# Multi-query attention with a SiLU feed-forward on one core: w1's load moved behind the transposes of x, the prologue replanned, other last rows for ScalarE and VectorE

## The chip, the core and the metric

The kernel runs on one core of a Trainium2 chip. The engines that matter here are TensorE (PE in the profile), VectorE (DVE), ScalarE (ACT), GpSimd (POOL) and SyncE (SP), which issues nearly all transfers. Each engine works through its own list of instructions in order, and the lists are tied together by semaphores. The metric is the device time of one execution in microseconds (us), as the median of several runs.

## The reference

The input x has 2048 rows of 640 columns. It is normalised by row, and the result feeds two branches whose outputs are added to x. Branch A is attention with 32 query heads of 20 columns and one shared key and value head; branch B is a feed-forward network with 1728 hidden columns.

```python
xn = _layernorm(x)                                   # (x - mean) / sqrt(var + 1e-5)
q = (xn @ wq).reshape(B, S, H, Dh).transpose(0, 2, 1, 3)
k, v = xn @ wk, xn @ wv                              # one head of 20 for all 32
p = softmax(einsum("bhqd,bkd->bhqk", q, k) * Dh ** -0.5)
o = einsum("bhqk,bkd->bhqd", p, v)
A = o.transpose(0, 2, 1, 3).reshape(B, S, H * Dh) @ wo
Bv = silu(xn @ w1) @ w2
out = x + A + Bv
```

## The kernel before

**Tiling.** The 2048 rows are 16 tiles of 128 rows (NT) and 4 chunks of 512 queries (QC). The scores of one head, one chunk of queries and one tile of 128 keys are a block of 128 keys by 512 queries; there are 32 x 4 x 16 = 2048 blocks. They are taken in groups of four heads (GB = 64 blocks), key tile by key tile, head by head inside a key tile. PE makes three (sometimes four) blocks at once (do_S, L1049, matmul L1101), each in one of PSUM's eight banks.

**Two ways to the exponential.** Most blocks go to ScalarE, which takes two or three banks in one instruction (L1135; here called a pair of 1024 columns, a triple of 1536, a single of 512). The others go to VectorE, which makes of the scores an integer whose bits are an approximate exponential (p1, L1150); two shifted copies of it are added by GpSimd (L1187) or VectorE (L1181), three blocks at a time. A block of ScalarE then costs one product with v on PE, a block of VectorE three (L942). Which blocks go to VectorE is decided block by block from its backlog (pick_dve, L974).

**Other work.** Once the sums of a group are complete, VectorE copies them out (L1231), a transfer transposes them (L1200), and VectorE and GpSimd divide by the row sums (L1215, L1220). Beside all this PE runs what is called jobs: q products for later heads (qd_job, L1268, followed by small transfers at L1290), hidden products of the feed-forward network with w1 (h_job, L1302, then tanh on ScalarE at L1324 and a product on VectorE at L1329), and output products (out_job, L1366). Products of this kind with 32 columns of weights are run four side by side (mm4, L840, matmul L844); four of them are called a quad here.

**What sets the order.** All of it is laid out when the kernel is built, by a list scheduler written in the kernel (Sched, L217). It knows a duration for each operation and a latency for each engine, and keeps a clock per engine; at each step the engine that is free first takes the ready operation of the best priority (run, L319; commit, L294). PE has its own choice (step, L683): scores if three banks are free, products with v, a job, or filler matmuls on zeros (fill, L784, matmul L820) that keep it busy. The result is one fixed list for each engine, and semaphore waits where an operation needs another engine's result (emit, L362). The row SEG (L115) sets the thresholds of these choices anew for every 32 blocks. The scheduler's times only decide the order; on the chip each engine goes on as soon as its waits are met.

**The prologue** (L1504). SP issues the loads of x, tile by tile (L1520), then wq (L1541), then w1 in five pieces (L1543), then transfers that transpose normalised tiles 4, 5 and 7 to 15 (L1704, "xTd"); then a fill of q's layout (qz, L1716) and the residual rows (L1461). The statistics of tiles 0, 4, 6, 9, 11 and 14 are made by ScalarE in two passes (L1610, L1613), the others by VectorE (L1625 twice, L1627). Three batches (tiles 0 to 3, 4 to 9, 10 to 15) each get a chain of small Newton operations on VectorE for 1/sqrt (newton, L1654), whose last operation makes -mean/std (L1683); a tile is then normalised as x * rstd + nb (norm, L1643) by VectorE, ScalarE (L1645) or GpSimd (L1650), as NORM_ENG says. Tiles 0 to 3 and 6 are transposed on PE (tr_job, L1735) and copied by ScalarE (0 and 2, L1747) or VectorE (L1750). k is made for two tiles at a time (k_job, L1754, copied by VectorE at L1766; GpSimd makes a second form of it for VectorE's blocks, L1768), v for four (v_job, L1773). The first q product, for four heads and 512 queries, is one job (q_job, L1246), copied by ScalarE (L1258). The jobs' order is the string PRO after a fixed start: four transposes, q, two k.

**The end.** The last chunk's output rows are four tiles in two halves each. For the first NEARLY tiles an earlier sum (the feed-forward part, x and the first columns of the attention output) is kept in SBUF, and VectorE adds the last products to it (L1412). For the other tiles, and the first HELD ones, a PSUM bank is held with the products made so far (hold_job, L1437); of the other tiles ScalarE copies the finished bank out (L1409). All need the last group, which is transposed on PE (L1238), normalised and copied (oT_last_job, L1350, copy L1361).

Of the kernel before, what the change touches and what calls it, by code (L numbers as in the profile page):

```python
# [15 lines left out]
P = 128  # L16
# [3 lines left out]
DC = 5  # L20
# [40 lines left out]
NEARLY = 3  # L61
EK = 3
HELD = 2
# [31 lines left out]
DVE_FROM = 3  # L95
NODB = 2
# [8 lines left out]
PRO = "v0 t6 k2 k3 v1 k4 q1 k5 v2 k6 k7 v3 d0"  # L105
ACT_STATS = (0, 4, 6, 9, 11, 14)
NW_ENG = ("dve", "dve", "dve")
NORM_ENG = ("pool", "pool", "pool", "pool", "dve", "dve", "act", "act", "pool", "pool", "act", "pool")
# [5 lines left out]
            "ACT4", "SPLIT", "U2")  # L114
SEG = (  # L115
    (4.7587, 0.6558, 0.636, 0.0937, 9, 3, 0, 1.3, 0.05, 0.63, 4.5, 24, 0.91, 1.3294, 10, 21, 8, 54, 22, 27, 99, 0, 0, 0, 99),
    (4.7587, 0.6558, 0.61, 0.112, 9, 3, 0, 1.3, 0.05, 0.6, 0.06, 24, 0.44, 1.3294, 0, 21, 8, 54, 24, 27, 99, 0, 0, 0, 99),
    (4.7587, 1.786, 0.633, 0.153, 7, 5, 3, 1.33, 0.05, 2.36, 0.03, 37, 2.01, 0.4, 10, 6, 5, 54, 15, 99, 99, 0, 0, 0, 99),
    (4.7587, 1.675, 0.488, 0.153, 7, 5, 3, 2.06, 0.05, 0.61, 0.03, 37, 2.01, 0.55, 10, 6, 5, 54, 15, 99, 99, 0, 0, 0, 99),
    (4.7587, 1.675, 0.633, 0.153, 7, 5, 3, 2.06, 0.05, 0.61, 0.03, 37, 2.01, 0.55, 10, 6, 5, 54, 15, 33, 99, 0, 0, 0, 99),  # L120
    (3.659, 1.675, 0.467, 0.034, 7, 5, 1, 1.98, 0.05, 0.41, 0.03, 34, 2.01, 0.55, 10, 6, 12, 54, 16, 33, 99, 0, 0, 0, 99),
    (3.659, 1.675, 0.576, 0.034, 7, 5, 1, 1.98, 0.05, 0.41, 0.03, 34, 2.01, 0.55, 10, 6, 12, 54, 16, 33, 99, 0, 0, 0, 99),
    (4.7587, 1.675, 0.633, 0.153, 7, 5, 3, 2.06, 0.05, 0.61, 0.03, 37, 3.09, 0.55, 10, 6, 5, 54, 15, 33, 99, 0, 0, 0, 99),
    (4.7587, 1.675, 0.633, 0.153, 7, 3, 3, 2.06, 0.05, 0.61, 0.03, 29, 3.09, 0.55, 10, 6, 5, 54, 15, 33, 9, 0, 0, 0, 99),
    (4.7587, 1.482, 0.633, 0.129, 9, 3, 1, 1.33, 0.05, 2.27, 4.5, 24, 0.89, 2.045, 10, 6, 7, 54, 22, 27, 99, 0, 0, 0, 99),
    (4.197, 0.657, 0.708, 0.288, 3, 1, 7, 0.02, 0.05, 4.23, 2.77, 26, 2.57, 1.233, 10, 7, 6, 54, 22, 99, 99, 0, 0, 0, 99),
# [57 lines left out]
class Op:  # L184
# [3 lines left out]
    def __init__(self, eng, dur, fn, deps, prio=0.0, name="", on_sched=None, mode=None):  # L188
# [21 lines left out]
        self.late = 0.0  # L210


LAT = {"pe": 0.215, "act": 0.238, "dve": 0.14, "pool": 0.19, "sp": 0.0}
INF = float("inf")


class Sched:  # L217
# [76 lines left out]
    def commit(self, op, start):  # L294
# [3 lines left out]
        if op.dma:  # L298
            if op.name in ("oTd", "xTd", "uTd"):
                self.dma_t = op.end  # L300
# [1570 lines left out]
```

## Time and profile before

| what | us |
| --- | --- |
| three runs | 683.74, 683.84, 687.07 |
| median | 683.84 |
| the profiled execution, its own time | 686.08 |
| its span, from the first to the last instruction | 684.3 |
| busy in the span: PE, ScalarE, VectorE, GpSimd | 673.0, 667.2, 610.8, 570.0 |
| exponentials on ScalarE (L1135), 649 instructions | 637.0 |
| blocks that VectorE takes (L1150), 687 | 456.5 |
| granted PE clock, mean | 0.994 |

The profile is of one execution. Busy time is the time in which an engine had an instruction at work; neighbours overlap, so a busy time over the count is more than the distance from one to the next. "Idle before" an instruction is shown with what ended it. The profiled execution took 686.08 us, of which 684.3 are the span and 1.8 lie around it.

### The profile page before, as it was taken

What the parts mean: (1) busy time and instruction counts of PE and PEld (TensorE: products, weight loads), DVE (VectorE), ACT (ScalarE), POOL (GpSimd) and SP (SyncE); (2) the same over time, 40 slices, a digit from 0 to 9 for tenths busy, and PEclk for the clock granted to TensorE, in tenths of its full rate; (3) what the DMA queues carried; (4) which work ended last, traced back from release to release, by engine and by line L of the source; (5) the groups of instructions that cost most, each with busy time, mean ns of one, the idle gap of its engine ahead of it and who ended that gap; (6) DMA issues with size and microseconds to landing.
All of it is one profiled execution on the core that took longest, in us unless ns stands there. A gap on an engine that the chain in (4) does not pass through costs nothing.

```text
span 684.3 us, 22554 instructions
## 1 busy us (share of the span) xinstructions
PE 673.0 (98%) x9632; PEld 225.2 (33%) x9634; DVE 610.8 (89%) x1088; ACT 667.2 (98%) x740; POOL 570.0 (83%) x450
## 2 busy tenths in 40 slices
PE   9799999999999999999999999999999999999997
PEld 4332222333323322333323322333332332233333
DVE  7689999888999998989999889988999999898996
ACT  7899999999999999999999999999999999999995
POOL 3567899789989999997798999899777998887692
PEclk9899999999999999999999999999999999999999
DMA  9735400000103100000002310000101220000101
GB/s 265 163 99 146 140 10 15 2 12 16 17 10 91 51 10 18 10 10 18 17 2 53 78 30 10 17 2 17 13 15 34 70 56 2 16 11 17 26 10 40
DMA packets 52728, 28.03 MB, mean 41 GB/s; under 512 B 38582, under 2 KB 51990, under 8 KB 52630
## 3 DMA queue, kind: packets, MB, share of 16 engines
q1 hardware_dynamic: 51174, 26.38, 15.2%
q8 instruction: 77, 1.26, 0.8%
q10 hardware_dynamic: 1456, 0.22, 0.2%
q14 instruction: 21, 0.17, 0.1%
HBM read 11.44 MB, written 2.62 MB: 21 GB/s over the span
## 4 chain that ended last, share of the span: by engine, by line
PE 65%; ACT 30%; DVE 3%; DMA 1%; issue 0%; POOL 0%; SPq 0%; DVEq 0%
ACT sbt L1135 28%; PE psall L942 23%; PE psall L1101 21%; PE psall L844 20%; ACT sbt L1324 2%; DVE sbt L1625 1%; DMA sbt<-sbt 1%; PE psall L1758 1%; DMA sbt<-in_A_x_dram 1%; PE psall L1314 0%; DVE sbt L1150 0%; POOL sbt L1650 0%; DVE sbt L1412 0%; DVE sbt L1650 0%; DVE sbt L1766 0%
## 5 line engine op out<-in xcount | busy, mean ns | idle before, releaser
L1135 ACT ACTIVATE sbt<-psall 128x1024 bf16<-128x1024 f32 (+1 forms) x649 | 637.0, 1177 | 4.8 <-PE psall L1101 4.1
L1187 POOL TENSOR_TENSOR sbt<-sbt 128x768 int32<-128x768 int32 x373 | 529.3, 1447 | 83.8 <-DVE sbt L1181 57.1
L1150 DVE TENSOR_SCALAR sbt<-psall 128x512 int16<-128x512 f32 x687 | 456.5, 685 | 51.9 <-PE psall L1101 44.0
L942 PE MATMUL psall<-sbt 128*32 128x512 bf16 x3422 | 265.1, 383 | 0.1
L1101 PE MATMUL psall<-sbt 32*128 32x512 bf16 x2048 | 252.8, 385 | 2.4 <-ACT sbt L1135 0.5
L844 PE MATMUL psall<-sbt 128*32 128x320 bf16 (+1 forms) x3903 | 231.9, 333 | 0.8 <-DVE sbt L1766 0.5
L1101 PEld LDWEIGHTS psall<-sbt 32*128 32x128 bf16 x2048 | 66.7, 91 | 249.0 <-issue 97.3
L844 PEld LDWEIGHTS psall<-sbt 128*32 128x32 bf16 x3903 | 81.9, 95 | 86.1 <-issue 62.2
L942 PEld LDWEIGHTS psall<-sbt 128*32 128x32 bf16 x3422 | 67.2, 95 | 99.4 <-issue 68.8
L1181 DVE TENSOR_SCALAR sbt<-sbt 128x1536 int16<-128x1536 int16 (+1 forms) x93 | 52.4, 574 | 0.2
L1324 ACT ACTIVATE sbt<-psall 128x512 bf16<-128x512 f32 x54 | 39.6, 732 | 0.0
L1329 DVE SCALAR_TENSOR_TENSOR sbt<-sbt,psall 128x512 bf16<-128x512 bf16 x54 | 37.0, 685 | 2.5 <-ACT sbt L1324 2.0
L1220 POOL TENSOR_TENSOR sbt<-sbt 128x320 bf16<-128x320 bf16 x31 | 22.6, 729 | 2.4 <-DVE sbt L1181 2.2
L1231 DVE CAST sbt<-psall 128x512 bf16<-128x512 f32 x32 | 21.8, 682 | 0.5 <-PE psall L942 0.3
L820 PE MATMUL psall<-sbt 128*128 128x512 bf16 (+3 forms) x53 | 15.7, 449 | 2.5 <-DVE sbt L1564 1.2
L1650 POOL TENSOR_SCALAR sbt<-sbt 128x640 bf16<-128x640 bf16 x7 | 6.0, 876 | 13.9 <-DVE sbt L1683 13.9
L1412 DVE SCALAR_TENSOR_TENSOR sbt<-psall,sbt 128x320 bf16<-128x320 f32 x30 | 14.1, 483 | 2.4 <-PE psall L844 2.3
L1281 DVE TENSOR_SCALAR sbt<-psall 128x512 bf16<-128x512 f32 (+1 forms) x19 | 12.9, 681 | 0.5 <-PE psall L844 0.5
L1393 DVE SCALAR_TENSOR_TENSOR sbt<-psall,sbt 128x320 bf16<-128x320 f32 x26 | 12.5, 482 | 0.8 <-PE psall L844 0.8
L1625 DVE BATCH_NORM_STATS2 sbt<-sbt 128x6 f32<-128x320 bf16 x20 | 9.2, 476 | 3.3 <-DMA sbt<-in_A_x_dram 3.3
L820 PEld LDWEIGHTS psall<-sbt 128*128 128x128 bf16 x55 | 6.0, 113 | 9.9 <-issue 4.0
L1758 PE MATMUL psall<-sbt 128*128 128x256 bf16 x40 | 7.0, 308 | 1.7 <-DMA sbt<-sbt 1.1
(71 smaller groups left out, 92.1 us busy)
## 6 DMA issues: line engine op xcount, KB each, us to landing
sbt<-in_A_x_dram SPq DMA_DIRECT2D x32, 160.0 KB, 3.4
out_dram<-sbt SPq DMA_DIRECT2D x15, 160.0 KB, 1.9
sbt<-in_B_w_dram SPq DMA_DIRECT2D x5, 432.0 KB, 6.7
sbt<-sbt SPq DMA_DIRECT2D x105, 20.0 KB
sbt<-in_B_w_dram SPq DMA_DIRECT2D x13, 160.0 KB, 3.2
sbt<-sbt SPq DMA_DIRECT2D x1, 1024.0 KB, 6.6
sbt<-sbt SPq DMA_TRANSPOSE x58, 2.5
sbt<-in_A_wo_dram SPq DMA_DIRECT2D x5, 160.0 KB, 3.1
```

What stands on the lines that cost most here:

```text
L820: return pe.matmul(self.bk(b, 0, n), self.zero[:, 0:P], self.zero[:, 0:n], start=True, stop=True)
L844: ins = pe.matmul(self.bk(b, 0, n, r, r + SLOT), w[:, r:r + SLOT], x, start=start, stop=stop, tile_position=(0, r), skip_group_check=True)
L942: ins = pe.matmul(self.bk(ub[k], 0, QW, r, r + SLOT), self.v[:, it.w, it.kt, :], it.x(), start=f, stop=False, tile_position=(0, r), skip_g ...
L1101: ins = pe.matmul(self.bk(bank[x]), self.kT[r:r + SLOT, kk, kt * P:(kt + 1) * P], self.qT[r:r + SLOT, g % 8, (g // 8) % 2, :], start=True, ...
L1135: return a.activation(self.E[:, b0 * QW:(b0 + na) * QW].rearrange("p (b n) -> p b n", n=QW), src, AF.Exp, scale=ACT_SCALE)
L1150: return v.tensor_scalar(self.Z[:, zs, zp * QW:(zp + 1) * QW], self.bk(bb), 0.0, ZMAX, ALU.max, ALU.min)
L1181: sc.new("dve", td, lambda v, k=k: v.tensor_scalar(self.Y[:, zs, k, 0:w], self.Z[:, zs, 0:w], float(PH[k + 1][0]), None, ALU.add), zk, yk, ...
L1187: sc.new("pool", tp, lambda v, k=k, cb=cb: v.tensor_tensor(self.Y[:, zs, k, 0:w].bitcast(I32), self.Z[:, zs, 0:w].bitcast(I32), cb, ALU.ad ...
L1220: op = sc.new(eng, 0.75 if eng == "pool" else t_dve_ps(16 * DH), lambda v: v.tensor_tensor(dst, ut[:, :, :, 0:DH], rb, ALU.mult), [key, (" ...
L1231: sc.new("dve", t_dve_ps(QW), lambda v: v.tensor_copy(self.U[:, up, :], self.bk(ub)), [("B", ub)], [("U", up)], prio=U_PRIO, name=f"Uev{g}")
L1324: sc.new("act", t_act(QW), lambda a: a.activation(t, src, AF.Tanh, scale=0.5), [("B", b)], [("tb", tp)], prio=TH_PRIO, name=f"th{c}_{fk}")
L1329: sc.new("dve", t_dve_ps(QW), lambda v: v.scalar_tensor_tensor(out=self.hT[0:rows, fk, :], in0=t, scalar=1.0, in1=src, op0=ALU.add, op1=AL ...
```

## The change

- w1's five loads go out on SP's queue after the transposes of x and the fill of q, instead of before them (load_w1).
- The string PRO now holds the whole order of the first jobs: two transposes, the first k product, two transposes, the first q product in two halves of 256 queries ("p0", "p1") with the second k product between them. k's product 4 stands ahead of v's second one.
- Tile 8 is normalised by GpSimd instead of VectorE, tile 12 by VectorE instead of GpSimd. VectorE and GpSimd normalise as (x - mean) * rstd; the operation that makes -mean/std is left out in batches of which ScalarE normalises no tile. The first norm is tied to the end of the first Newton chain.
- The scheduler's assumptions: a time for each transfer by its queue (dmaq), a start time for each engine, PE's latency 0.222 instead of 0.215, a later result for tanh, 0.69 for GpSimd's normalisation. A setting LOOK lets an engine hold off for an operation of better priority; it is 0 in all rows of SEG.
- Of the last chunk two tiles (four half rows) are finished by ScalarE and two by VectorE, instead of one and three; no held banks for the first tiles.
- Most rows of SEG have other values.

In the built kernel the blocks divide into 1364 for ScalarE (579 pairs, 68 triples, 2 singles) and 684 for VectorE; before, 1361 (576, 68, 5) and 687. The long run of work between prologue and end has another order throughout.

```diff
 H_FIRST = 4
-NEARLY = 3
+NEARLY = 2
 EK = 3
-HELD = 2
+HELD = 0
...
 DVE_FROM = 3
+Q0_SPLIT = 1
+W1_LATE = 1
...
 PV_GO = 9
-PRO = "v0 t6 k2 k3 v1 k4 q1 k5 v2 k6 k7 v3 d0"
+PRO = "t0 t1 k0 t2 t3 p0 k1 p1 v0 t6 k2 k3 k4 v1 q1 k5 v2 k6 k7 v3 d0"
...
 NW_ENG = ("dve", "dve", "dve")
-NORM_ENG = ("pool", "pool", "pool", "pool", "dve", "dve", "act", "act", "pool", "pool", "act", "pool")
+NORM_ENG = ("pool", "pool", "pool", "pool", "pool", "dve", "act", "act", "dve", "pool", "act", "pool")
...
             "ZWAIT", "Y0_POOL", "Y0_COST", "JOB_BURST", "TILE_CAP", "E_HIGH", "Q_LEAD", "U_GO", "U_Z", "JU_E", "STRETCH",
-            "ACT4", "SPLIT", "U2")
+            "ACT4", "SPLIT", "U2", "LOOK")
...
-LAT = {"pe": 0.215, "act": 0.238, "dve": 0.14, "pool": 0.19, "sp": 0.0}
+LAT = {"pe": 0.222, "act": 0.238, "dve": 0.14, "pool": 0.19, "sp": 0.0}
...
         self.order = {e: [] for e in self.engs}
-        self.t = {e: 0.0 for e in self.engs}
+        self.t = {"pe": 1.1, "act": 0.7, "dve": 0.8, "pool": 0.7, "sp": 0.7}
...
         self.last_add = None
+        self.dmaq = defaultdict(float)
...
         if op.dma:
+            q = self.dmaq[e]
             if op.name in ("oTd", "xTd", "uTd"):
-                self.dma_t = op.end
-            self.dma_t = max(getattr(self, "dma_t", 0.0), op.end) + op.mode / 230e3
-            op.avail = op.end + 1.6 + op.late if op.name in ("oTd", "xTd", "uTd") else max(op.end + 2.0, self.dma_t + 1.6)
+                op.avail = max(op.end + (1.2 if op.name == "xTd" else 1.6) + op.late, q + 0.8)
+            else:
+                op.avail = max(op.end + 2.0, q + op.mode / 375e3)
+            self.dmaq[e] = max(q, op.avail - op.late)
         else:
-            op.avail = op.end + LAT[e]
+            op.avail = op.end + LAT[e] + op.late
...
                 self.last_add = op
-            self.lock_end[e] = op.end + (LAT["dve"] if e == "dve" else 0.0)
+            self.lock_end[e] = op.end + (0.2 if e == "dve" else 0.0)
...
     def run(self):
-        wake = {e: 0.0 for e in self.engs}
+        wake = dict(self.t)
...
                 nxt = INF
+                soon = []
...
                             best = (key, op)
-                    elif r < nxt:
-                        nxt = r
+                    else:
+                        nxt = min(nxt, r)
+                        if r < now + LOOK:
+                            soon.append((r, op.prio))
+                if best is not None and e != "sp":
+                    r = min((r for r, p in soon if p < best[0][0] - 0.3 and r < now + best[1].dur), default=INF)
+                    if r < INF:
+                        best, nxt = None, r
...
         if c == 0 and h < 8:
-            return [("q", c, h, 0)]
+            return [("q", c, h, 0), ("q", c, h, 256)]
...
         rb = bass.AP(self.rL, rl.offset, [list(rl.ap[0]), list(rl.ap[1]), [1, 4], [0, DH]])
-        op = sc.new(eng, 0.75 if eng == "pool" else t_dve_ps(16 * DH), lambda v: v.tensor_tensor(
+        op = sc.new(eng, 0.69 if eng == "pool" else t_dve_ps(16 * DH), lambda v: v.tensor_tensor(
...
-    def q_job(self, ht, act=False):
+    def q_job(self, ht, act=False, lo=0, hi=QW):
...
             def f(pe, b, k=k):
-                return self.mm4(pe, b, QW, self.wqp[:, k, ht * P:(ht + 1) * P], self.xnT[:, k, 0:QW], k == 0, k == DC - 1)
-            mms.append((t_mm(QW), f))
+                return self.mm4(pe, b, hi - lo, self.wqp[:, k, ht * P:(ht + 1) * P], self.xnT[:, k, lo:hi], k == 0, k == DC - 1)
+            mms.append((t_mm(hi - lo), f))
...
         def consume(b):
-            dst = self.qT[:, ht, 0, :]
-            ks = [("q", 0, h, 0) for h in range(4 * ht, 4 * ht + 4)] + [("qb", 0, h) for h in range(4 * ht, 4 * ht + 4)]
+            dst = self.qT[:, ht, 0, lo:hi]
+            ks = [("q", 0, h, a) for h in range(4 * ht, 4 * ht + 4) for a in (0, 256) if lo <= a < hi]
+            ks += [("qb", 0, h) for h in range(4 * ht, 4 * ht + 4)]
             if act:
-                sc.new("act", t_act(QW), lambda a: a.activation(dst, self.bk(b), AF.Identity, bias=self.offq[:, :],
+                sc.new("act", t_act(hi - lo), lambda a: a.activation(dst, self.bk(b, 0, hi - lo), AF.Identity, bias=self.offq[:, :],
...
                        [("B", b), ("offq",)], ks, prio=X_PRIO, name=f"qev0_{ht}")
-        reads = [("xnT", i) for i in range(4)] + [("wq", ht)] + [("oT", i) for i in range(4)]
-        return Job(f"q0_{ht}", mms, reads, consume, width=QW, n=4, mode="PV")
+        reads = [("xnT", i) for i in range(lo // P, hi // P)] + [("wq", ht)] + [("oT", i) for i in range(4)]
+        return Job(f"q0_{ht}", mms, reads, consume, width=hi - lo, n=4, mode="PV")
...
             sc.new("act", t_act(QW), lambda a: a.activation(t, src, AF.Tanh, scale=0.5), [("B", b)], [("tb", tp)],
-                   prio=TH_PRIO, name=f"th{c}_{fk}")
+                   prio=TH_PRIO, name=f"th{c}_{fk}").late = 0.06
...
                            for c in range(DC)], ("wqd", 1), P * D * 2)
-        load_w("sp", "1", [lambda q, c=c: q.dma_start(self.w1[:, c, :], self.B_w1[c * P:(c + 1) * P, :])
-                           for c in range(DC)], ("w1",), P * F * 2)
+        def load_w1():
+            load_w("sp", "1", [lambda q, c=c: q.dma_start(self.w1[:, c, :], self.B_w1[c * P:(c + 1) * P, :])
+                               for c in range(DC)], ("w1",), P * F * 2)
+        if not W1_LATE:
+            load_w1()
...
                 return
-            np_(eng, 0.36 if eng == "dve" else 0.87, lambda v: v.tensor_scalar(
-                xa(n), self.xslot(n), self.rstd[:, n:n + 1], self.nb[:, n:n + 1], ALU.mult, ALU.add),
-                self.xkeys(n) + [("nb", n), ("rs", ra)], [("xn", n)], prio=prio, name=f"norm{n}").lock = True
+            op = np_(eng, 0.36 if eng == "dve" else 0.87, lambda v: v.tensor_scalar(
+                xa(n), self.xslot(n), self.mv[:, n, 0:1], self.rstd[:, n:n + 1], ALU.subtract, ALU.mult),
+                self.xkeys(n) + [("mv", n), ("rs", ra)], [("xn", n)], prio=prio, name=f"norm{n}")
+            op.lock = True
+            if n == 0 and self.last_nw.eng == eng:
+                self.last_nw.then = op
...
                 ch[-1].lock = True
+                self.last_nw = ch[-1]
...
                     nw(lambda v: v.tensor_tensor(y_, w_, y_, ALU.mult), rw + rr, rr)
+            if not any(NORM_ENG[n - 4] == "act" for n in range(max(a, 4), b_)):
+                return
...
         qz(0)
+        if W1_LATE:
+            load_w1()
...
-        for n in range(4):
-            self.pro.append(tr_job(n))
-        self.pro.append(self.q_job(0, act=True))
-        self.pro.append(k_job(0))
-        self.pro.append(k_job(1))
...
             n = int(w[1:])
-            self.pro.append(tr_job(n) if w[0] == "t" else k_job(n) if w[0] == "k" else self.q_job(n)
-                             if w[0] == "q" else self.qd_job(0, n) if w[0] == "d" else v_job(4 * n, 4 * n + 4))
+            self.pro.append(tr_job(n) if w[0] == "t" else k_job(n) if w[0] == "k" else self.q_job(n, n == 0)
+                             if w[0] == "q" else self.q_job(0, True, 256 * n, 256 * n + 256) if w[0] == "p" else self.qd_job(0, n) if w[0] == "d" else v_job(4 * n, 4 * n + 4))
```

## The prediction

> **What bounds the kernel now.** I read the page's busy shares first, then ScalarE's waits and its order of time, then what PE, VectorE and SP did around its gaps, then the tail. ScalarE is busy 667.2 us of 684.3.
>
> ```profile
> ACT sbt L1409 <- PE psall L844: 4.3, 1, 4.3
> ACT sbt L1135 <- PE psall L1101: 4.1, 6, 1.7
> ```
>
> These are ScalarE's waits of any size: one in the tail, six in its exponentials, nearly all before 42 us. In order of time (start, length, instructions, idle before):
>
> ```profile
> 17.61 0.52 ACT L1599 ACTIVATE sbt<-sbt 128x400 bf16<-128x400 bf16 x1
> 18.07 5.68 ACT L1135 ACTIVATE sbt<-psall 128x1536 bf16<-128x1536 f32 x4
> 25.45 1.02 ACT L1135 ACTIVATE sbt<-psall 128x1024 bf16<-128x1024 f32 x1 [1.70 <-PE psall L1101]
> 26.38 2.53 ACT L1645 ACTIVATE sbt<-sbt 128x640 bf16<-128x640 bf16 x3
> 28.81 2.34 ACT L1135 ACTIVATE sbt<-psall 128x1024 bf16<-128x1024 f32 x2
> 31.73 1.02 ACT L1135 ACTIVATE sbt<-psall 128x1024 bf16<-128x1024 f32 x1 [0.58 <-PE psall L1101]
> 33.68 1.02 ACT L1135 ACTIVATE sbt<-psall 128x1024 bf16<-128x1024 f32 x1 [0.92 <-PE psall L1101]
> 34.93 6.52 ACT L1135 ACTIVATE sbt<-psall 128x1024 bf16<-128x1024 f32 x7 [0.22 <-PE psall L1101]
> 41.94 17.95 ACT L1135 ACTIVATE sbt<-psall 128x1536 bf16<-128x1536 f32 x19 [0.49 <-PE psall L1101]
> ```
>
> From 42 us to the last exponential, which ends at 674.97, ScalarE hardly stops. So the end is: start of the first exponential (18.07), plus ScalarE's own work, plus gaps, plus a tail of 684.3 - 674.97 = 9.3. Its prices follow from the ends of rows: seven pairs take 6.52, with 0.10 of the first one's longer run off 0.917 each; a tanh of 512 columns adds 0.49. The early gaps sum to 1.70 + 0.58 + 0.92 + 0.22 + 0.49 = 3.9, and each also costs about 0.1 since a lone pair takes 1.02, not 0.917: 4.4.
>
> What made them:
>
> ```profile
> 24.07 0.80 PE L1758 MATMUL psall<-sbt 128*128 128x256 bf16 x3 [1.05 <-DMA sbt<-sbt]
> 17.64 0.60 PE L1101 MATMUL psall<-sbt 32*128 32x512 bf16 x6
> 17.01 0.17 DVE L1683 SCALAR_TENSOR_TENSOR sbt<-sbt 128x6 f32<-128x6 f32 x1
> 17.09 0.75 DVE L1766 CAST sbt<-psall 128x256 bf16<-128x256 f32 x2
> DMA to landing us min/median/max: 2.4/2.5/4.6
> DMA to landing us min/median/max: 4.9/6.7/8.9
> ```
>
> PE stood before the k product of tiles 4 and 5 until their transposes had landed; the next scores (24.80) were queued behind it. The first landing line is the eleven transposes of L1704: the slowest 4.6 us, the median 2.5. The second is w1 (L1543), issued on the same queue at 11.2 to 14.0 us, so its slowest piece landed about 13.1 + 8.9 = 22.0. The first transposes went out at 18.18 and 19.58 into that. And the first scores (17.64) waited for k, whose copies (17.09) stood behind VectorE's second Newton chain (15.41 to 17.1).
>
> **The first exponential.** From 10.98 to 18.07 ScalarE works without a stop: 7.09 us. In the changed order tile 9's mean pass comes ahead of the copy of tile 0, so it fills the 0.89 that ScalarE waited there: -0.72 (start to start, 11.58 to 12.30). wq's second copy moves behind five exponentials: -0.46 (17.61 to 18.07). The q copy becomes two of 256 columns. No row has that shape: from 512 and 1024 columns (0.49, 0.917) a line gives 0.28 each, +0.06; were each as long as the 512 one here (0.57), +0.57; I take +0.1, nearer the line. On VectorE the Newton chain loses its last operation (0.20) but both halves of tile 5's statistics (0.40 each) now stand ahead of it, one in place of the half that stood behind it; the first norm starts some 0.07 later than 9.78. The regrouping lets a sum of squares be followed by a copy that need not wait for it: -0.1. Together 18.07 - 1.2 = 16.9. Is PE in time? k's copy now precedes the Newton chain; the transposed tile 3 is copied by 14.1, k's second product takes 0.55, the second half of q 0.55, its copy is done at about 16.1, and scores to exponential took 18.07 - 17.64 = 0.43: 16.6, so ScalarE's own queue decides. The norms' other form, (x - mean) times rstd, has the same shape and as many operands (0.36 on VectorE, 0.86 on GpSimd); I take no change, a gain is excluded, and the far end is the rate of L1625 (0.40 for 320 columns, so 0.80): 4 x 0.44 = 1.8 later.
>
> **The gaps after it.** w1 now goes out behind all eleven transposes and the 768 KB fill of q. With 2.45 to land, as the undisturbed ones took, tile 5 is there at 22.0 instead of 23.9. What decides more is that ScalarE runs five triples (15 of the 16 blocks that the first two k products serve), then wq's copy and its three norms (2.43) in one piece: 16.9 + 5 x 1.36 + 0.46 + 2.43 = 26.6. The norms' inputs come from the third Newton chain, some 0.9 sooner than at 24.9 since less stands ahead of it. In that time PE gets tiles 4 to 7, VectorE copies k right behind the Newton chain (about 24.5), and six blocks of scores lie ready at 25.2: the gap of 1.70 goes, with 1.4 to spare. Two triples then give PE 2.7 us for the products of tiles 8, 9 and v; tiles 10 and 11 leave ScalarE two us earlier. I keep 0.7 of the 4.4: -3.7. If every gap went, -4.4; if the four later ones stayed (2.2 and their 0.4), -1.8.
>
> **Work added to ScalarE.** As built, the changed kernel has 579 pairs, 68 triples and 2 singles for 576, 68 and 5: 3 x 0.917 - 3 x 0.49 = +1.3. wq's copy, now after the first exponential: +0.46. Together +1.75. VectorE gets 684 blocks instead of 687, PE as many score products, 3416 second products for 3422, and 2464 products of 320 columns for 2448; both have room on the way (VectorE is 89% busy).
>
> **w1 later.** Issued at about 34 to 36.5 us, behind SP's transposes, whose last waits for GpSimd's and ScalarE's norms; behind it wait the four loads of residual rows and q's copies (first at 51.7 before). The first product that reads w1 came before the tanh at 59.69; at 26.6 plus 4 triples and 26 pairs the changed tanh stands at 56, its product about 55. Even with 8.9 to land and the fill of q ahead (5.5) w1 is there by 45. Cover: 10 us. Without it ScalarE stops for each us that is missing, since PE takes its queue in order.
>
> **The tail.** PE runs without a stop from the last scores to its end. Lines at the end:
>
> ```profile
> 676.77 1.27 PE L844 MATMUL psall<-sbt 128*32 128x320 bf16 x32
> 678.41 0.42 DVE L1361 COPY sbt<-psall 128x512 bf16<-128x512 bf16 x1 [0.75 <-PE psall L1356]
> 679.26 0.97 ACT L1409 ACTIVATE sbt<-psall 128x320 bf16<-128x320 f32 x2 [4.28 <-PE psall L844]
> 679.46 2.48 DVE L1412 SCALAR_TENSOR_TENSOR sbt<-psall,sbt 128x320 bf16<-128x320 f32 x6 [0.63 <-PE psall L844]
> ```
>
> Call C the time when PE may use the last copy (678.97). The six VectorE rows end at 681.94 = C + 3.0. In the changed order 48 products of 0.037 follow C instead of 40, two quads to each VectorE half, one to each ScalarE half; VectorE's four start at C + 0.64 and then each 0.44: end C + 2.4, -0.5. ScalarE's four end at C + 2.05, beside them. Ahead of C the fillers change from 32, 32 and 8 to 28, 24 and 24: -0.15, -0.2 (VectorE's norm then decides) and +0.2. Sum -0.7; bounds -1.1 and 0, if PE's longer queue eats what the shorter evacuation gives.
>
> **Sum:** -1.2 - 3.7 + 1.75 - 0.7 = -3.9 against the profiled execution. That one took 686.08 for its span of 684.3 (1.8 around it), 2.2 over the median of 683.84; I take the difference off the median: 679.9.
>
> **Rivals.**
> A cold PE (B). In 2 us windows (length, busy time of PE, PEld, DVE, ACT, POOL, then the clock) PE idled while it waited, and the clock fell:
>
> ```profile
> 20.00:22.00 2.00, 0.84 (x9) 0.40 (x9) 2.00 (x9) 2.00 (x2) 1.65 (x3) 1.00 1.07 139
> 22.00:24.00 2.00, 1.01 (x6) 0.28 (x3) 1.83 (x9) 1.66 (x2) 0.00 (x0) 1.00 1.21 178
> 24.00:26.00 2.00, 1.93 (x9) 0.82 (x10) 0.80 (x6) 0.55 (x1) 0.98 (x2) 0.50 0.68 153
> ```
>
> At that clock scores reached ScalarE after 0.65 (24.80 to 25.45) instead of 0.43, and q's product of 12 took 1.47 instead of 0.83. The changed order also idles PE, before tile 5 lands and while ScalarE norms, so the four later gaps may stay: -1.2 - 1.8 + 1.75 - 0.7 = -1.95, 681.9. Against: ScalarE has 2.7 us of triples in hand there. (The Trainium skill, "TensorE: Matmul & The Clock Gate", section "What's actually happening", says that the array runs at half clock after about one idle window of 3.4 us and at full clock after one busy window; the granted 0.50 above agrees with the half, and by that rule B would hold wherever the new order idles PE that long.)
>
> The change doesn't do what it says (C): the gaps belonged to the profiled execution, which is 2.2 over the median, and the timed runs have only half of them to lose: -1.2 - 1.5 + 1.75 - 0.7 = -1.65, 682.2. For it: that 2.2 has no other place in the trace. Against: the waits have a structural cause.
>
> Slower (D): the order of some 9600 matmuls between 42 and 670 us is new. Before, the ends and starts of ScalarE's neighbouring rows show six waits for PE there, 0.05 to 0.2 each, about 0.8 in all. If the new order makes PE stand before banks that VectorE still empties at one score step in 16 of some 640, 40 waits of 0.15 add 6: 679.9 + 6 = 685.9. It decides from 26 such waits on. Against: work per engine is the same within half a per cent, and ScalarE has been the last one throughout.
>
> **Numbers.** Forecast (A) 0.58, own range 678.4 to 681.4; B 0.22; C 0.12; D 0.08. About 0.5% (3.4 us, so below 680.4) is what a measurement can tell from no change: of A some seven tenths lie below it, of B and C a sixth: faster 0.46, same 0.47, slower 0.07. The 80% range runs from 678.0 to 684.2: its lower end has all gaps gone and the better tail, its upper end the slow norms with B, and leaves out most of D.
>
> **What will show it.** First exponential near 16.9; no idle of ScalarE before the three norms; the first transposes landing 2.5 after issue; early gaps under 1; last evacuation 2.4 after C. Wrong if ScalarE idles over 2 us between 25 and 42, or if many short waits show after that.

## Result and the profile after

The changed kernel took 691.00 us (median of 6 runs, 689.36 to 692.34), the kernel before 684.83 beside it (6 runs, 683.08 to 687.07): a ratio of 1.0089, 95% interval 1.0062 to 1.0116. It is slower; 679.9 was forecast, and 691.0 lies outside the range of 678.0 to 684.2. The profiled execution of the changed kernel took 689.36 for a span of 687.5 and is the fastest of its six, while the profile of before is of a long execution; so the two profiles differ by less (3.3) than the medians (6.2).

ScalarE's waits in the profile after (us in total, times, longest):

```profile
ACT sbt L1147 <- PE psall L1113: 7.2, 5, 4.6
ACT sbt L1422 <- PE psall L856: 4.2, 1, 4.2
ACT sbt L1661 <- DVE sbt L1705: 0.5, 1, 0.5
```

The waits for scores were 4.1 and are 7.2, one alone 4.6. In order of time (start, length, then the idle time before):

```profile
16.73 5.46 ACT L1147 ACTIVATE sbt<-psall 128x1536 bf16<-128x1536 f32 x4
26.74 1.45 ACT L1147 ACTIVATE sbt<-psall 128x1536 bf16<-128x1536 f32 x1 [4.55 <-PE psall L1113]
28.09 0.53 ACT L1615 ACTIVATE sbt<-sbt 128x400 bf16<-128x400 bf16 x1
29.11 2.54 ACT L1661 ACTIVATE sbt<-sbt 128x640 bf16<-128x640 bf16 x3 [0.50 <-DVE sbt L1705]
31.56 2.76 ACT L1147 ACTIVATE sbt<-psall 128x1536 bf16<-128x1536 f32 x2
35.86 1.02 ACT L1147 ACTIVATE sbt<-psall 128x1024 bf16<-128x1024 f32 x1 [1.54 <-PE psall L1113]
37.16 23.88 ACT L1147 ACTIVATE sbt<-psall 128x1024 bf16<-128x1024 f32 x25 [0.28 <-PE psall L1113]
```

The first exponential starts 1.34 earlier, as forecast. Then ScalarE stands for 4.55 after four triples and for 1.54 later on. What it waited for is found two steps back, in the rows of PE, GpSimd and VectorE of the same stretch:

```profile
17.06 17.39 POOL L1666 TENSOR_SCALAR sbt<-sbt 128x640 bf16<-128x640 bf16 x7 [3.26 <-DVE sbt L1696]
34.44 1.84 POOL L1792 TENSOR_SCALAR sbt<-sbt 128x256 bf16<-128x256 bf16 x4
...
24.59 0.71 PE L1763 MATMUL psall<-sbt 128*128 128x128 bf16 x5 [4.30 <-POOL sbt L1666]
33.35 0.71 PE L1782 MATMUL psall<-sbt 128*128 128x256 bf16 x5 [1.53 <-DMA sbt<-sbt]
...
25.34 0.49 DVE L1774 COPY sbt<-psall 128x640 bf16<-128x640 bf16 x1 [3.98 <-PE psall L1763]
```

PE's transposition of tile 6 (L1763) waited 4.30 for GpSimd's norm of that tile; the scores stood behind it in PE's queue. VectorE waited 3.98 for that transposition, and with it the third Newton chain, which gives ScalarE's three norms their input. GpSimd ran its seven norms from 17.06 to 34.45 without a stop; the transfers of the later tiles, PE's k products (the wait of 1.53) and GpSimd's own copies of k (34.44) followed at that pace. The groups of the two pages show why (busy us, mean ns of one, idle before). Before:

```profile
L1650 POOL TENSOR_SCALAR sbt<-sbt 128x640 bf16<-128x640 bf16 x7 | 6.0, 876 | 13.9 <-DVE sbt L1683 13.9
```

After:

```profile
L1666 POOL TENSOR_SCALAR sbt<-sbt 128x640 bf16<-128x640 bf16 x7 | 17.4, 2498 | 3.3 <-DVE sbt L1696 3.3
```

Same engine, same shape, same count, same number of operands: 876 ns became 2498. What differs is the pair of operations, (mult, add) before and (subtract, mult) after, and with it the two per-row values that they take; e1 and e4 below tell these apart. VectorE's four first norms, which made the same switch, took 1.51 together (1.50 before). The clock in 2 us windows (columns as in the prediction: PE's busy time first, the clock third from the end):

```profile
20.00:22.00 2.00, 0.29 (x3) 0.00 (x0) 1.36 (x6) 2.00 (x2) 2.00 (x1) 1.00 0.36 82
22.00:24.00 2.00, 0.00 (x0) 0.00 (x0) 0.00 (x0) 0.19 (x1) 2.00 (x2) 1.00 0.36 82
24.00:26.00 2.00, 1.41 (x7) 0.66 (x7) 0.66 (x3) 0.00 (x0) 2.00 (x2) 0.55 0.00 0
```

PE stood still for 4.3 us, and in the next window the granted clock was 0.55; in before it was 0.50 after PE's waits. The transfers themselves were as forecast: the eleven transposes landed 2.4 to 4.1 after issue, w1, now behind them, 5.0 to 6.4, and the trace has no instruction that waited for w1:

```profile
DMA to landing us min/median/max: 2.4/2.5/4.1
DMA to landing us min/median/max: 5.0/5.4/6.4
```

The tail:

```profile
681.59 2.63 PE L856 MATMUL psall<-sbt 128*32 128x320 bf16 x72
681.70 0.42 DVE L1374 COPY sbt<-psall 128x512 bf16<-128x512 bf16 x1 [0.49 <-PE psall L1369]
682.84 1.72 ACT L1422 ACTIVATE sbt<-psall 128x320 bf16<-128x320 f32 x4 [4.18 <-PE psall L856]
683.12 1.71 DVE L1425 SCALAR_TENSOR_TENSOR sbt<-psall,sbt 128x320 bf16<-128x320 f32 x4 [1.00 <-PE psall L856]
```

The spans by the prediction's terms. "Early" and "later" gaps are ScalarE's idle times over 0.04 before and after 60 us; "work" is what is left between the first and the last exponential; the tail runs from the end of the last exponential to the end of the span. Two kernels of the experiments below stand beside them; both of their profiles are of short executions (682.65 and 683.42 us, where the medians are 684.43 and 684.79).

| | before | after | after - before | before, a short execution (e5) | change with fast norms (e6) | e6 - e5 |
| --- | --- | --- | --- | --- | --- | --- |
| first exponential | 18.07 | 16.73 | -1.34 | 18.09 | 16.79 | -1.30 |
| early gaps | 4.01 | 6.87 | +2.86 | 0.90 | 0.15 | -0.75 |
| later gaps | 0.76 | 1.27 | +0.51 | 0.75 | 2.00 | +1.25 |
| work | 652.13 | 653.78 | +1.65 | 651.77 | 653.69 | +1.92 |
| tail | 9.31 | 8.90 | -0.41 | 9.31 | 8.94 | -0.37 |
| span | 684.28 | 687.55 | +3.27 | 680.82 | 681.56 | +0.74 |

### The profile page after: what moved, and what is told of

Read it like the earlier page. It is cut to its first block, busy times and chain, and to the rows that moved or that the text cites. A ratio compares the mean times of both kernels' runs of the same rounds, so it can differ in the third digit from the quotient of the medians.

```text
span 687.5 us, 22602 instructions
## 1 busy us (share of the span) xinstructions
PE 672.0 (98%) x9665; PEld 224.8 (33%) x9668; DVE 609.8 (89%) x1077; ACT 668.9 (97%) x743; POOL 580.4 (84%) x450
## 4 chain that ended last, share of the span: by engine, by line
PE 68%; ACT 26%; POOL 3%; DVE 2%; DMA 1%; issue 0%; SPq 0%; DVEq 0%
ACT sbt L1147 24%; PE psall L954 24%; PE psall L1113 23%; PE psall L856 21%; POOL sbt L1666 3%; ACT sbt L1337 1%; DVE sbt L1641 1%; DMA sbt<-in_A_x_dram 1%; PE psall L1327 0%; DVE sbt L1666 0%; DVE sbt L1193 0%; DVE sbt L1162 0%; DVE sbt L1425 0%; PE psall L823 0%; POOL sbt L1792 0%
## 5 line engine op out<-in xcount | busy, mean ns | idle before, releaser
L1147 ACT ACTIVATE sbt<-psall 128x1024 bf16<-128x1024 f32 (+1 forms) x649 | 637.7, 1171 | 7.7 <-PE psall L1113 7.2
L1199 POOL TENSOR_TENSOR sbt<-sbt 128x768 int32<-128x768 int32 (+2 forms) x373 | 528.6, 1444 | 78.7 <-DVE sbt L1193 54.5
L954 PE MATMUL psall<-sbt 128*32 128x512 bf16 x3416 | 260.3, 383 | 0.4 <-DVE sbt L1193 0.4
L856 PE MATMUL psall<-sbt 128*32 128x320 bf16 (+2 forms) x3939 | 234.1, 331 | 0.2
L1193 DVE TENSOR_SCALAR sbt<-sbt 128x1536 int16<-128x1536 int16 (+2 forms) x91 | 54.1, 601 | 0.3
L1666 POOL TENSOR_SCALAR sbt<-sbt 128x640 bf16<-128x640 bf16 x7 | 17.4, 2498 | 3.3 <-DVE sbt L1696 3.3
L832 PE MATMUL psall<-sbt 128*128 128x512 bf16 (+4 forms) x52 | 16.5, 459 | 1.7 <-DVE sbt L1580 1.2
L1792 POOL TENSOR_SCALAR sbt<-sbt 128x256 bf16<-128x256 bf16 x8 | 3.7, 479 | 9.7 <-DVE sbt L1790 9.6
```

The source lines that it names most:

```text
L832: return pe.matmul(self.bk(b, 0, n), self.zero[:, 0:P], self.zero[:, 0:n], start=True, stop=True)
L856: ins = pe.matmul(self.bk(b, 0, n, r, r + SLOT), w[:, r:r + SLOT], x, start=start, stop=stop, tile_position=(0, r), skip_group_check=True)
L954: ins = pe.matmul(self.bk(ub[k], 0, QW, r, r + SLOT), self.v[:, it.w, it.kt, :], it.x(), start=f, stop=False, tile_position=(0, r), skip_g ...
L1147: return a.activation(self.E[:, b0 * QW:(b0 + na) * QW].rearrange("p (b n) -> p b n", n=QW), src, AF.Exp, scale=ACT_SCALE)
L1193: sc.new("dve", td, lambda v, k=k: v.tensor_scalar(self.Y[:, zs, k, 0:w], self.Z[:, zs, 0:w], float(PH[k + 1][0]), None, ALU.add), zk, yk, ...
L1199: sc.new("pool", tp, lambda v, k=k, cb=cb: v.tensor_tensor(self.Y[:, zs, k, 0:w].bitcast(I32), self.Z[:, zs, 0:w].bitcast(I32), cb, ALU.ad ...
```

## The experiments

Two questions: is it the form of the norm on GpSimd, or the new order; and, if the form, why the rest of the change does not give the 3.9 that the prediction summed.

**e1: the changed kernel with the old pair of operations on GpSimd.** The edit, in the norm:

```diff
-                xa(n), self.xslot(n), self.mv[:, n, 0:1], self.rstd[:, n:n + 1], ALU.subtract, ALU.mult),
+                xa(n), self.xslot(n), *((self.rstd[:, n:n + 1], self.mv[:, n, 0:1], ALU.mult, ALU.add) if eng == "pool" else
+                                        (self.mv[:, n, 0:1], self.rstd[:, n:n + 1], ALU.subtract, ALU.mult))),
```

> The changed kernel, instruction for instruction, except that GpSimd's seven norms are (x mult rstd) add mean instead of (x subtract mean) mult rstd: the same two operands in the other pair of operations. In those seven tiles the mean is added where the reference subtracts mean times rstd, so the values differ. Theory N (the form of the norm costs on GpSimd, 2.50 us where the other form took 0.87): the seven take 0.87 each, GpSimd is through with them near 23.2 instead of 34.45, PE's wait of 4.30 for them and ScalarE's wait of 4.55 at 26.74 go, ScalarE's idle time between 16 and 60 us falls from 6.87 to under 1.5, and the time is 5 to 6 under the run of the changed kernel (687.5 of span to 681.5 to 682.5), so 2 to 3 below before. Rival O (the order is what is late: w1 behind the transposes, the norms of all tiles in a row, short waits of the new plan): the idle time stays above 5 and the time stays within 1.5 of the changed kernel, above 686.

Measured: 684.38 us (12 runs, 683.15 to 686.93), before 684.60 beside it, ratio 0.9992 (0.9969 to 1.0015). The seven norms took 874 ns each, and the early gaps are 1.02. The gap of 4.55 and the 1.54 are gone: against the changed kernel's 691.00 the form costs 6.6 us, the whole loss against before. Theory N holds in its mechanism. Its time was two too low: the kernel is level with before, not 2 to 3 below, since that was counted between two profiled executions of which one was short and the other long.

**e2: the kernel before with the new pair of operations on GpSimd alone.**

```diff
-                xa(n), self.xslot(n), self.rstd[:, n:n + 1], self.nb[:, n:n + 1], ALU.mult, ALU.add),
+                xa(n), self.xslot(n), *((self.mv[:, n, 0:1], self.rstd[:, n:n + 1], ALU.subtract, ALU.mult) if eng == "pool" else
+                                        (self.rstd[:, n:n + 1], self.nb[:, n:n + 1], ALU.mult, ALU.add))),
```

> The kernel before, in its own order, with GpSimd's seven norms alone in the new form, (x subtract mean) mult rstd. Theory N: each takes 2.50 instead of 0.87, so four from 17.3 end at 27.3 instead of 20.7, three more and the copies of k behind them about 8 to 11 later than in before; ScalarE waits for them in the first stage and the time is 4 to 9 above before. Rival O: the norms take 0.87 to 1.0 or their delay is covered, and the time is within 1 of before.

Measured: 694.09 (6 runs, 692.51 to 695.92), ratio 1.0134 (1.0102 to 1.0167): 9.5 slower with nothing else touched, a little over the 4 to 9 of theory N. GpSimd's rows of this kernel:

```profile
17.47 10.04 POOL L1650 TENSOR_SCALAR sbt<-sbt 128x640 bf16<-128x640 bf16 x4 [10.70 <-DVE sbt L1684]
27.49 0.92 POOL L1769 TENSOR_SCALAR sbt<-sbt 128x256 bf16<-128x256 bf16 x2
29.73 7.46 POOL L1650 TENSOR_SCALAR sbt<-sbt 128x640 bf16<-128x640 bf16 x3 [1.32 <-DVE sbt L1684]
```

The four norms of the kernel before:

```profile
17.29 3.45 POOL L1650 TENSOR_SCALAR sbt<-sbt 128x640 bf16<-128x640 bf16 x4 [10.49 <-DVE sbt L1683]
```

Four norms take 10.04 instead of 3.45, the copies of k come behind them, and the early gaps are 13.2. So the cost does not depend on the new order. In the new order the same form costs less (6.6 against 9.5); why was not tried.

**e4: which part of the pair is dear.** The changed kernel with another pair in each of the seven norms:

```diff
+    return {4: (r, m, ALU.mult, ALU.subtract), 5: (m, r, ALU.add, ALU.mult), 6: (m, r, ALU.subtract, ALU.mult),
+            7: (r, m, ALU.mult, ALU.add), 8: (m, 20.0, ALU.subtract, ALU.mult), 13: (m, None, ALU.subtract),
+            15: (0.0, 20.0, ALU.subtract, ALU.mult)}[n]
```

> The changed kernel with a different pair of operations in each of GpSimd's norms, to see which ingredient is dear; those tiles' values are not the reference's. Tile 4 mult rstd, subtract mean; 5 add mean, mult rstd; 6 subtract mean, mult rstd (as in the changed kernel); 7 mult rstd, add mean; 8 subtract mean, mult by the constant 20; 13 subtract mean alone; 15 subtract 0, mult 20, both constants. If subtract as an operation is dear, 4, 6, 8, 13 and 15 take about 2.5 and 5 and 7 about 0.87; if it is subtract ahead of mult, 6, 8 and 15; if it is an addition ahead of a multiplication by a per-row value, 5 and 6; if it is where the operands lie (the mean's column of the statistics), 4 to 8 and 13 all are. For the time there is no expectation.

GpSimd's rows in order of time, so tiles 4, 5, 6, 7, 8, 13 and 15:

```profile
17.27 2.50 POOL L1672 TENSOR_SCALAR sbt<-sbt 128x640 bf16<-128x640 bf16 x1 [3.25 <-DVE sbt L1703]
19.77 0.87 POOL L1672 TENSOR_SCALAR sbt<-sbt 128x640 bf16<-128x640 bf16 x1
20.61 2.51 POOL L1672 TENSOR_SCALAR sbt<-sbt 128x640 bf16<-128x640 bf16 x1
23.11 0.88 POOL L1672 TENSOR_SCALAR sbt<-sbt 128x640 bf16<-128x640 bf16 x1
24.08 2.42 POOL L1672 TENSOR_SCALAR sbt<-sbt 128x640 bf16<-128x640 bf16 x1
26.82 1.89 POOL L1672 TENSOR_SCALAR sbt<-sbt 128x640 bf16<-128x640 bf16 x1 [0.33 <-DVE sbt L1712]
30.51 2.35 POOL L1672 TENSOR_SCALAR sbt<-sbt 128x640 bf16<-128x640 bf16 x1 [1.80 <-DVE sbt L1672]
```

Every one with a subtract is slow, in first or second place, with a value per row or with constants, and even alone (1.89). Both with add and mult take 0.87, with the same operands and in either order. It is the subtraction, not the operands' place or number. The time of this run, 689.83, decides nothing.

**e3: the whole change with (x mult rstd) add nb on GpSimd, planned anew.** One more VectorE instruction of 0.09 stands in a Newton chain, and the planner lays everything out again:

```diff
-                xa(n), self.xslot(n), self.mv[:, n, 0:1], self.rstd[:, n:n + 1], ALU.subtract, ALU.mult),
+                xa(n), self.xslot(n), *((self.rstd[:, n:n + 1], self.nb[:, n:n + 1], ALU.mult, ALU.add) if eng == "pool" else
...
-            if not any(NORM_ENG[n - 4] == "act" for n in range(max(a, 4), b_)):
+            if not any(NORM_ENG[n - 4] != "dve" for n in range(max(a, 4), b_)):
```

> The changed kernel with GpSimd's norms as (x mult rstd) add nb, as before, with the products nb = -mean times rstd made by one more small VectorE instruction per batch that has a GpSimd norm; all values as the reference has them. The planner lays the rest out anew, so late parts differ in order. Theory N: norms 0.87 each, ScalarE's idle time between 16 and 60 under 2, time 679 to 683, below before by 2 to 5. Rival O: 686 or more, as the changed kernel.

Measured: 703.92 (6 runs), ratio 1.0276 (1.0245 to 1.0306), a miss for both theories. The norms took 874 ns and the early gaps are 1.22, so the cause lies elsewhere. This is its wait row of ScalarE, which has 29 waits instead of 5:

```profile
ACT sbt L1147 <- PE psall L1113: 14.4, 29, 2.6
```

Most of them lie between 72 and 660 us, and ScalarE got 664 exponentials instead of 649 (642.4 us of them for 637.7). With norms as short and the order kept, e1 and e6 take 684.4 and 684.8, so the other order costs 19 us. The likely reading is that the rows of SEG were set for one order and that the planner, shifted by 0.1 us, makes other choices throughout; which of them cost the time was not followed up. From here on the order of every queue was kept by hand.

**e6: the whole change, exact values, order kept.** GpSimd adds the negated mean, then multiplies; VectorE makes the negated means inside the last Newton step, at no cost to the planner:

```diff
+                xa(n), self.xslot(n), *((self.ex2[:, n:n + 1], self.rstd[:, n:n + 1], ALU.add, ALU.mult) if eng == "pool" else
...
+                def last_two(v, f=ch[-1].fn):
+                    v.tensor_scalar(self.ex2[:, a:b_], m_, -1.0, None, ALU.mult)
+                    return f(v)
+                ch[-1].fn = last_two
```

> The changed kernel with the planner's order of every engine kept, whose GpSimd norms are (x add the negated mean) mult rstd; the negated means of a batch come from one more VectorE instruction of six columns (about 0.09 us) ahead of the last step of each of the second and third Newton chains. All values as the reference has them. Theory N: seven norms of 0.87, the same time as with the mult, add norms in this order, 683.5 to 685.5, 6 to 7 below the changed kernel. Rival O' (the order itself cannot bear a small shift; the third kernel's 703.9 came from the 0.1 us on the chain): 690 or more. Against before: theory C makes it level within 1.5.

Measured: 684.79 (12 runs, 683.42 to 686.04), before 684.43 beside it, ratio 1.0003 (0.9990 to 1.0015). ScalarE's rows after the first exponential:

```profile
16.79 6.80 ACT L1147 ACTIVATE sbt<-psall 128x1536 bf16<-128x1536 f32 x5
23.43 0.57 ACT L1615 ACTIVATE sbt<-sbt 128x400 bf16<-128x400 bf16 x1
24.16 2.54 ACT L1661 ACTIVATE sbt<-sbt 128x640 bf16<-128x640 bf16 x3
26.60 29.19 ACT L1147 ACTIVATE sbt<-psall 128x1536 bf16<-128x1536 f32 x30
```

Five triples, wq's copy and three norms in one piece to 26.6, which is what the prediction described, and only 0.15 of early gaps. And still it is level with before.

**e5: the kernel before, unchanged, profiled again.**

> The kernel before, unchanged, for a second profile. The profile that the prediction was summed from is of an execution 2.2 us over the median, with a granted clock of 0.994. Theory C (part of the early gaps belongs to that execution): in an execution of granted clock 0.997 or more, with a span near 682, ScalarE's idle time from the first exponential to 60 us is 1 to 2.5, not 4.01, and PE's granted clock in 25 to 35 us is well above 0.71. Rival (the gaps are in every execution): 3.7 to 4.3 again and the difference lies elsewhere.

This execution took 682.65, span 680.8, granted clock 0.999. It is a short one: of the 69 timed executions of before beside these runs, whose median is 684.51, only one took less. ScalarE's rows, then PE's k product of tiles 4 and 5:

```profile
18.09 5.57 ACT L1135 ACTIVATE sbt<-psall 128x1536 bf16<-128x1536 f32 x4
24.06 1.02 ACT L1135 ACTIVATE sbt<-psall 128x1024 bf16<-128x1024 f32 x1 [0.40 <-PE psall L1101]
24.98 2.53 ACT L1645 ACTIVATE sbt<-sbt 128x640 bf16<-128x640 bf16 x3
27.41 10.56 ACT L1135 ACTIVATE sbt<-psall 128x1024 bf16<-128x1024 f32 x11
38.47 17.95 ACT L1135 ACTIVATE sbt<-psall 128x1536 bf16<-128x1536 f32 x19 [0.50 <-PE psall L1101]
...
23.20 0.49 PE L1758 MATMUL psall<-sbt 128*128 128x256 bf16 x3 [0.28 <-DMA sbt<-sbt]
```

Against the first profile of before: PE's wait for the transposes is 0.28, not 1.05; the clock holds 1.00 from 25 to 35 us, not 0.71; the gaps of 1.70, 0.58, 0.92 and 0.22 are one of 0.40. The early gaps are 0.90, not 4.01. Theory C holds for this execution, a little more strongly than stated, but an ordinary one lies between the two profiles. So does the profile of e9 (below), whose order is that of before up to the last 40 us. Its execution took 685.22, of which 1.5 are a late write at the end, and its early gaps are 2.01, most of it in this row:

```profile
25.11 1.02 ACT L1135 ACTIVATE sbt<-psall 128x1024 bf16<-128x1024 f32 x1 [1.35 <-PE psall L1101]
```

From these three profiles (0.90 at 682.7, 2.01 at 683.7 without the late write, 4.01 at 686.1) I estimate 2 to 3 us of early gaps for an ordinary execution of 684.5. The 69 timed executions point the same way: 14 with a granted clock of 0.999 or more took 682.6 to 683.7 us, 23 at 0.997 and 0.998 took 683.4 to 685.0, 21 at 0.994 to 0.996 took 683.7 to 686.3, 11 at 0.992 or less 686.6 to 689.9. (The Trainium skill, "TensorE: Matmul & The Clock Gate", section "What's actually happening", says that the window by which the clock is set runs freely, so that one kernel can see different cold stretches from run to run. The two profiles of before agree with that as far as they go; no run here shows the window itself.)

**e7 and e8: w1's place alone.** In e7 w1 goes back ahead of the transposes in the kernel of e6; in e8 it goes behind them in the kernel before. Only SP's order changes (this is e8's edit; e7's sets the loads just ahead of the first transpose in the same way):

```diff
+        sp = b.sc.order["sp"]
+        last = max(op.start for op in sp if op.name == "xTd")
+        for i, op in enumerate([op for op in sp if op.mode == P * F * 2]):
+            op.start = last + 1e-4 * (i + 1)
+            op.end = op.start
         lists = b.sc.emit()
```

> The kernel just named with the five loads of w1 put back ahead of the eleven transposes in SP's queue, every other order the same. Theory W (moving w1 is worth what the prediction gave it): the transposes start about 3.5 later or land behind 2.2 MB of w1, products of k wait for them, ScalarE idles 2 to 5 more before 45 us, the time rises by 2 to 5. Rival: with GpSimd's norms at 0.87 SP waits for norms rather than for its own issues; the rise is under 1.

> The kernel before, every order the same, with the five loads of w1 put behind the eleven transposes in SP's queue: that part of the change alone. Theory W: transposes land 2 to 4 earlier, the early gaps of before shrink, time 1 to 3 below before. Theory C: in ordinary executions there is little of these gaps to win, so 0 to 1.5 below. Rival P (the products of k and v that come free sooner stand in front of scores in PE's fixed order, or x slots' reload waits for w1's issues): 0 to 2 above.

Measured: e7 683.92 (12 runs), ratio to before 0.9997 (0.9984 to 1.0011), beside 684.79 of e6: not 2 to 5 slower, if anything faster. Its transposes started 0.27 later and landed in 2.4 to 4.1 (2.4 to 4.2 in e6), and its early gaps are nothing. e8 684.10, ratio 0.9993 (0.9980 to 1.0007): within theory C's 0 to 1.5 below, but level by its interval. In e8's trace the transposes landed 2.4 to 4.1 after issue, in e5's, with w1 ahead of them, 2.4 to 4.0. Theory W falls: by itself w1's place is worth nothing that can be measured here, where the intervals reach about 1 us to either side.

**e9 and e10: the tail alone.** The two settings in the kernel before, and their undoing in the kernel of e6:

```diff
-NEARLY = 3
+NEARLY = 2
-HELD = 2
+HELD = 0
```

> The kernel before with the change's tail alone (two rows of the last four held instead of three and two, four of the last eight half rows evacuated by ScalarE and four by VectorE); everything ahead of the last 40 us is in the same order. The prediction gave the tail -0.7; the two profiles gave 9.31 to 8.90, -0.41. Theory T: tail (from the end of the last exponential to the end of the span) 8.85 to 9.05, time 0.3 to 0.5 below before. Rival: two rows' last products more behind the last transposition on PE (96 of 320 columns instead of 48) cost what the split saves, tail 9.2 to 9.4, time level.

> The whole change with GpSimd's norms as (x add the negated mean) mult rstd and the order kept, but with the tail of before. Theory T: tail 9.2 to 9.4 where that kernel had 8.94, span up by 0.3 to 0.5 at the same granted clock. Rival: 8.9 to 9.0.

e9: 684.70 (12 runs), ratio 1.0004 (0.9979 to 1.0029). There 96 products of 320 columns stand behind the last transposition, for 72 in the changed kernel and 48 in before. The tail in its trace is 10.86, outside both expectations. The products did not make it so long: VectorE's last row ends 6.89 after the last exponential, in before 6.97. From that row to the end of the span it is 3.97, because the last two writes landed late. In e11, which has the same tail, VectorE's last row ends at 6.89 too, and 2.48 follow, so that the tail is 9.37. The landing of the last two writes, in e9 and in e11:

```profile
DMA to landing us min/median/max: 3.3/3.4/3.5
DMA to landing us min/median/max: 1.8/1.9/2.0
```

So in the order of before the new tail gains nothing (9.37 for 9.31, by one trace), and the 1.5 more of e9 belong to one execution. e10 is the fair pair: span 682.21, tail 9.16 for e6's 8.94, so the new tail is worth 0.2 there, half of what theory T said. (The span itself is 0.65 longer; most of the rest is later gaps, 2.56 for 2.00.) From the last exponential to VectorE's last row it is 6.83 in e10 and 6.19 in e6, 0.64 less; from that row to the end of the span it is 2.33 and 2.75, 0.42 more.

**e11: both parts that leave the order of before alone,** e8's edit and e9's.

> The kernel before with two parts of the change that leave its order alone: w1's loads behind the eleven transposes, and the new tail. In the run with w1 behind alone 11 of 12 executions had a granted clock of 0.997 or more, and of before 23 of 46. Theory C (the stretch in which PE falls to half clock is set off by a late transpose, and w1 behind them makes that rarer): at least 10 of 12 executions at 0.997 or more, median 683.3 to 684.0, 0.5 to 1.0 below before and below the changed kernel with its norms mended. Rival: the 11 of 12 were chance; half of the executions at 0.997 or more, median within 0.4 of before.

Measured: 685.11 (12 runs), ratio 1.0016 (0.9998 to 1.0034); 8 of 12 executions at 0.997 or more, and of all 69 of before 37. A miss for theory C. With e8's 11 of 12 it makes 19 of 24, so whether w1's place makes the long executions rarer in the order of before stays open; no version of these runs beats before.

## Why the prediction was wrong

**The step that failed** is the norm's other form: "the same shape and as many operands (0.36 on VectorE, 0.86 on GpSimd); I take no change". For VectorE that was right. For GpSimd the price was carried over from a row with other operations, and the only bound that was worked out (1.8) was for VectorE's four norms; GpSimd's seven had none. They cost 2.50 instead of 0.87, 11.4 us of GpSimd's time, and 6.2 to 6.6 us of the kernel's (691.00 against e6 and e1). No row of before had a subtraction on GpSimd, so the trace could not have given the price; a bound from "no such row" would have been wide. The sign of being wrong that the prediction named, over 2 us of ScalarE's idle time between 25 and 42, came with 4.1.

**First exponential:** 16.9 forecast, 16.73 measured. Right.

**The gaps after it** are a second error, hidden by the first. The order does what was described, as e6 shows (26.60 for 26.6, 0.15 idle before the three norms). But -3.7 was measured on one long execution and taken off the median of all. Where that one has 4.01, the short execution of e5 has 0.90, of which e6's, short too, wins 0.75. An ordinary one has 2 to 3 by the estimate above, and the changed kernel with norms of 0.87 has 1.02 in e1's profile, of an execution near its median (684.97 and 684.38). So in ordinary executions the term is worth 1 to 2 and not 3.7. This is rival C, which got 0.12: its price of -1.5 for this term was about right, and so was its reason, that the 2.2 over the median have no other place in the trace; "the waits have a structural cause" did not outweigh it. Rival B had described how such a gap comes about: a late transfer, a PE that stands, then a low clock (0.50 in before). But B expected that of the new order, and the late transfer isn't needed: in e9 no product waited for one, PE stood 1.16 before 21.54 for VectorE, in e5 1.08, and yet the granted clock from 22 to 26 was 0.57 in e9 and 1.00 in e5. Of the 36 timed executions of e1, e6 and e7, with w1 behind the transposes or ahead of them, 34 had a granted clock of 0.997 or more, of before 37 of 69. So with norms of 0.87 the new order has the long executions more rarely; what it wins there it loses in the work and the later gaps.

**Work added:** +1.75 forecast, +1.65 and +1.92 by the two pairs of profiles. Right.

**Later gaps** had no term. They grow by 0.51 and 1.25; in e6 two make most of it, 0.45 at 73.8 and 0.80 at 80.9. Rival D was about many short waits there; there were 5 waits for scores in all in the profile after. Its 685.9 is nearer to 691.0 than the forecast, by another mechanism. What delays these two scores was read from one trace (PE waiting for GpSimd and VectorE just ahead) and not tried.

**Tail:** -0.7 forecast, -0.41 and -0.37 measured. By e6, VectorE's last row ends at C + 2.57 (2.4 forecast) and the stretch ahead of C is 0.38 shorter (0.15 forecast). So the part that was summed came to -0.8; the term left out is the end of the output's writes, 0.41 longer. The last write took 2.2 from issue to landing in after and e6, and 1.7 in before, e5 and e10; the last four writes start within 1.2 us in the former and within 1.7 in the latter. Whether that closeness is the cause was not tried.

**w1 later:** the cover held. Nothing waited for it in the traces of after, e1, e6, e7 and e8; the transposes' slowest landing fell from 4.6 to 4.1, but it was 4.0 in e5 too, with w1 ahead of them, and e7 shows that ScalarE did not wait for this.

**The sum, put right:** between the two short executions (e6 against e5) -1.30 - 0.75 + 1.25 + 1.92 - 0.37 = +0.75, and then some 6 for the norms. With 1 to 2 for the early gaps of ordinary executions in place of the 0.75 it comes to between +0.5 and -0.5, and the medians of e6 and before are level (ratio 1.0003). Of the miss of 11.1 somewhat more than half is the norms' price. In the rest, by the short executions the sum's -3.9 against +0.75, the early gaps are 2.95, the later ones 1.25, the tail 0.33 and the work 0.17.

## What to carry to other kernels

The price of an instruction belongs to its engine and its operations, not to its shape alone: when a change swaps the operations on an engine whose rows don't show the new ones, run that one instruction first, or give it a bound wide enough to be the forecast's largest. A gap seen in one profile is worth its mean over the executions, so when the profiled one is above the median by as much as the gaps that are to be won, profile one near the median before summing; one well below it misleads in the other direction. An order tuned row by row should be changed by hand at the point in question: letting the planner lay it out anew for 0.1 us cost 19.

## What the runs showed of the hardware

On GpSimd a subtraction over 128x640 bf16 took 1.89 us alone and 2.35 to 2.51 in a pair, and the pairs of add and mult 0.87, with values per row in either order; VectorE's four norms took 1.51 with the subtraction and 1.50 without. So GpSimd takes 2.3 times VectorE's 0.38 (1.51 / 4) in one form and 6.6 times in the other. (The Trainium skill, "GPSIMD Engine Reference", section "3.1 Elementwise — side-by-side cycle accounting", gives GpSimd about twice VectorE's time, for an addition of two tensors. The rows with add and mult are near that; those with a subtraction are not.) Adding a negated value does the same work: e6 computes what the reference does and has the 0.87.
